# S4D convolution plus Mish feed-forward on one Trainium2 core: a new order for the first three chunks of block 0

## The chip, the core and the metric

The kernel runs on one core of a Trainium2 chip. A core has a matrix engine (PE; its weight loads are listed as PEld), a vector engine (DVE), an activation engine (ACT), a general engine (POOL) and a sync engine (SP) that mainly issues DMAs. Each engine works through its own instruction stream in order; semaphores tie the streams together. Matrix products end in PSUM, everything else lies in SBUF. The metric is the device time of one execution in microseconds. A time is the median of several runs, and one more execution is profiled; all traces here come from such a profiled execution.

## The reference

The input `A_u` is 2048 rows of 640. It is normalized per row, and three terms are added: the input itself, a diagonal state-space convolution with a skip term, and a dense layer pair with Mish between.

```python
x = A_u
xn = _layernorm(x, axis=-1)
return x + _A_ref(xn, ...) + _B_ref(xn, B_w1, B_b1, B_w2)

def _B_ref(x, w1, b1, w2):
    h = jnp.einsum("bsd,df->bsf", x, w1) + b1
    sp = jnp.log1p(jnp.exp(-jnp.abs(h))) + jnp.where(h > 0, h, jnp.zeros_like(h))
    act = h * jnp.tanh(sp)
    return jnp.einsum("bsf,fd->bsd", act, w2)
```

The inner width of the dense pair is 1728. The work in question is the beginning of `_layernorm` and of the first `einsum`.

## The kernel before

**Tiling.** The 2048 rows are four blocks of 512. A block has four tiles of 128 rows, numbered 0 to 3. The 640 columns are five slices `k`, the 1728 inner columns 14 chunks `f` (thirteen of 128, one of 64). PE multiplies 16-bit floats: each 32-bit operand is split into a rounded part, "high", and the residual, "low", and a product of two operands is made of three: high x high (`hh`), low weights x high input (`lh`), high weights x low input (`hl`). A chunk of the first layer thus has 15 products 512 columns wide, or 30 of half that width, called halves below; `CA` is the first half of a block's columns (tiles 0 and 1), `CB` the second (tiles 2 and 3).

**Two regimes.** From chunk 3 of block 0 on, a planner (`Plan`) orders all engines. It gets an estimated start time per engine, costs, predecessors and due times, and lets each engine take what is ready and due. PE's own order is that in which its operations were added. A predecessor that already has an entry in `pl.end` is dropped when an operation is added (`add`, line 89). The beginning, chunks 0, 1 and 2 of block 0, is an order written out by hand under `tc.manual_schedule()` (lines 1253 to 1334): each engine gets its instructions in the order of the calls.

**The steps of the beginning.** For every tile `i` of block 0:
- the tile is loaded to `X0`: tiles 0 and 1 as two column halves, one on SP's queue and one on ACT's (1256, 1257), tiles 2 and 3 as two halves of 64 rows on the same two queues (`load_x0`, 1245)
- DVE makes the statistics, two passes over half the columns each and a merge (`stat_ops`, 625), adds the epsilon (1280), and POOL raises the variance to the power -0.5 (1281)
- DVE subtracts the mean and multiplies (`norm0`, 1220); a variant on ACT, `norm0_a` (1223), exists but is not called
- PE transposes the five slices into PSUM (`to_t0`, 1235), slice 4 first.

For each half of the columns and each slice ACT copies the transposed input to 16 bits (`hi0`, 1239) and DVE makes the residual (`lo0`, 1242). For each chunk, `load_w1` (533) brings the weights, ACT rounds them (`hi_w1`, 550) and DVE makes their residual (`lo_w1`, 554). `mm1_part` (784) then issues products for a chunk, a list of kinds, a half and a list of slices. PE also runs 11 products of no use at the start (`fill`, 1249). In the old order chunks 1 and 2 do their low-weight products over all 512 columns at once.

**Loads.** Those of the weights of chunks 0 and 1 are split between SP's and ACT's queues as are those of all four tiles; ACT issues six DMAs before its first activation `warm` (1266), which makes it load its function tables. The rest goes out on SP.

**What follows.** Chunk 3 of the first layer is the first product at line 807, and after it PE alternates second-layer products (859) with further chunks. The first second-layer products wait for the activation of chunk 0: sigmoid (890), product with the input (894), arctangent, square and hyperbolic tangent on ACT (898, 902, 906), product (910) and split (916, 926).

Of the kernel before, what the change touches and what calls it, by code (L numbers as in the profile page):

```python
# [16 lines left out]
AF = mybir.ActivationFunctionType  # L17
OP = mybir.AluOpType
AX = mybir.AxisListType

P = 128
L = 2048
# [3 lines left out]
TB = 512  # L26
NB = L // TB
NT = TB // P
KD = D // P
# [9 lines left out]
EPS = 1e-5  # L39
# [10 lines left out]
SX, S1, SA, S2 = 2.0 ** 8, 2.0 ** 14, 2.0 ** 8, 2.0 ** 16  # L50
# [402 lines left out]
def body(ctx: ExitStack, tc: tile.TileContext, x, xT, logA, Aim, Cr, Ci, logdt, vec, w1, w1T, w2, w2T, out):  # L453
    nc = tc.nc
    v, a, pe, sp, g = nc.vector, nc.scalar, nc.tensor, nc.sync, nc.gpsimd
    xr = x[0].rearrange("(b i p) d -> b i p d", b=NB, i=NT, p=P)
# [10 lines left out]
    row = pool("row", 1)  # L467
# [11 lines left out]
    half, one, pi4, mb, zero = (kc[:, i:i + 1] for i in range(5))  # L479
    warm = kc[:, 5:6]  # L480
# [25 lines left out]
    CA, CB = slice(0, TB // 2), slice(TB // 2, TB)  # L506
# [10 lines left out]
    ACC = [ps.tile([P, TB], F32, name=f"acc{k}") for k in range(KD)]  # L517
    XT, ACT, SM, NX = ({} for _ in range(4))
    NCHK = NF + 3 * KD
    pl = Plan({"PE": 20.8, "ACT": 16.1, "DVE": 17.9, "SP": 15.0, "POOL": 15.0})  # L520
    tiles = lambda pool, name, n, shape: [pool.tile(shape, F32, name=f"{name}{j}") for j in range(n)]
    pl.pool("w", tiles(row, "w", 8, [P, D]))
    pl.pool("x", tiles(row, "x", 2, [P, D]))
# [9 lines left out]
    def load_w1(f, queues=(sp,)):  # L533
        t = kf(pl["w1", f])
        n, m = FC[f], P // len(queues)
        for j, e in enumerate(queues):
            o = D * FO[f] + j * m * KD * n
            e.dma_start(t[j * m:(j + 1) * m, :, :n], w1[o:o + m * KD * n].rearrange("(p k f) -> p k f", p=m, k=KD))
# [11 lines left out]
    def hi_w1(f):  # L550
        n = FC[f]
        a.activation(W1H[f][:, :, :n], kf(pl["w1", f])[:, :, :n], AF.Copy, scale=S1)

    def lo_w1(f):
        n = FC[f]
        v.scalar_tensor_tensor(W1L[f], kf(pl["w1", f])[:, :, :n], S1, W1H[f][:, :, :n], op0=OP.mult, op1=OP.subtract)
# [68 lines left out]
    def stat_ops(mv, xt, i):  # L625
        st = tmp.tile([P, 2, 6], F32, name="st", bufs=2)
        yield lambda: v.bn_stats(st[:, 0], xt[:, 0:320])  # L627
        yield lambda: v.bn_stats(st[:, 1], xt[:, 320:640])  # L628
        yield lambda: v.bn_aggr(mv[:, i], st)
# [154 lines left out]
    def mm1_part(f, kinds, c, start=False, stop=False, ks=range(KD)):  # L784

        ops = {"hh": (W1H[f], XH[0]), "lh": (W1L[f], XH[0]), "hl": (W1H[f], XL[0])}
        seq = [(ops[o], k) for k in ks for o in kinds]
        for j, ((w, x), k) in enumerate(seq):
            pe.matmul(bank(0, f)[:, c], w[:, k], x[k][:, c], start=start and j == 0, stop=stop and j == len(seq) - 1)  # L789
# [146 lines left out]
    def whole():  # L936

        A, V, M, S, G = "ACT", "DVE", "PE", "SP", "POOL"
        M5, M2 = 0.2157, 0.11
# [45 lines left out]
            return ops  # L985

        for f in range(3):
            pl.end["m1", 0, f] = (16.95, 18.55, 20.75)[f]


        for f in range(NF):
            if f > 5:
                add(("lw1", f), S, 0.1, load_w1, f, take=("w", ("w1", f), 1), kb=327.0)
            if f > 3:
                add(("hw1", f), A, 0.65, hi_w1, f, pre=[("lw1", f)] if f > 5 else [])
                add(("ow1", f), V, 0.75, lo_w1, f, pre=[("hw1", f)], drop=[("w1", f)])
            if f > 1:
                add(("lw2", f), S, 0.1, load_w2, f, take=("w", ("w2", f), 1), kb=327.0)
            add(("hw2", f), A, 0.65, hi_w2, f, pre=[("lw2", f)] if f > 1 else [])
# [17 lines left out]
        for b in range(1, NB):  # L1017
            for f in range(NF):
# [13 lines left out]
                i = PAIRS.index(f)  # L1032
                c = b
                one, two, three_a, three_b, four = mm1_pair(b, f)
# [12 lines left out]
                A2, B2 = second(*g2, [9] if FC[g2[1]] == P else [6]), second(*h2, [3, 9] if FC[h2[1]] == P else [2, 6])  # L1047
# [25 lines left out]
        b, k = NB - 1, KD - 1  # L1073
        two, one = LAST - 2, LAST - 1
# [25 lines left out]
        start = lambda b, f: at.get(("m1", b, f)) or at.get(("one", b, f)) or (start(b, f - 1) if f else pl.t["PE"] - 3.0)  # L1100

        for c in range(1, NB):
            b = c - 1
            t0 = start(b, 0)
            for i in range(NT):
                add(("lx", c, i), S, 0.1, lambda c=c, i=i: sp.dma_start(pl["x", c, i], xr[c, i]),
                    pre=[("st", c, i - 2)] if i > 1 else [], take=("x", ("x", c, i), 1), rel=t0, kb=327.0)
                add(("st", c, i), V, 1.1, stats, c, i, pre=[("lx", c, i)] + [("st", c, i - 1)] * (i > 0), drop=[("x", c, i)])
            add(("rs", c), G, 2.6, rstds, pre=[("st", c, NT - 1)])
            add(("sr", c), A, 0.25, spread_a, pre=[("spread", c)])  # L1110
            add(("sd", c), S, 0.1, spread_d, pre=[("sr", c)], kb=4.0)
            add(("bc", c), S, 0.2, spread_l, c, pre=[("sd", c)], take=("b", ("b", c), 2 * KD), kb=512.0)
# [103 lines left out]
    X0 = big.tile([P, NT, D], F32, name="x0", tag="bigA")  # L1216
    mv0 = tmp.tile([P, NT, 2], F32, name="mv0")
    rs0 = tmp.tile([P, 2, NT], F32, name="rs0")

    def norm0(i):  # L1220
        v.tensor_scalar(X0[:, i], X0[:, i], mv0[:, i, 0:1], rs0[:, 0, i:i + 1], op0=OP.subtract, op1=OP.mult)

    def norm0_a(i):
        v.scalar_tensor_tensor(rs0[:, 1, i:i + 1], mv0[:, i:i + 1, 0], -1.0, rs0[:, 0, i:i + 1], op0=OP.mult, op1=OP.mult)
        a.activation(X0[:, i], X0[:, i], AF.Identity, bias=rs0[:, 1, i:i + 1], scale=rs0[:, 0, i:i + 1])


    KS = (KD - 1, *range(KD - 1))
# [6 lines left out]
    def to_t0(i):  # L1235
        for k in KS:
            pe.transpose(flat0(k, (CA, CB)[i // 2])[:, i % 2 * P:(i % 2 + 1) * P], X0[:, i, k * P:(k + 1) * P], ident)  # L1237

    def hi0(k, c):
        a.activation(XH[0][k][:, c], flat0(k, c), AF.Copy, scale=SX)  # L1240

    def lo0(k, c):
        v.scalar_tensor_tensor(XL[0][k][:, c], flat0(k, c), SX, XH[0][k][:, c], op0=OP.mult, op1=OP.subtract)

    def load_x0(i):
        for e, c in ((sp, slice(0, P // 2)), (a, slice(P // 2, P))):
            e.dma_start(X0[c, i], xr[0, i, c])

    def fill(n):
        for _ in range(n):  # L1250
            pe.matmul(TR[:, 0:P], ident, ident, start=True, stop=True)

    with tc.manual_schedule():

        for i in range(2):
            sp.dma_start(X0[:, i, 0:320], xr[0, i, :, 0:320])
            a.dma_start(X0[:, i, 320:D], xr[0, i, :, 320:D])  # L1257
        for f in range(6):
            pl.take("w", ("w1", f))
            if f < 2:  # L1260
                pl.take("w", ("w2", f))
        load_w1(0, (sp, a))
        load_x0(2)
        load_w1(1, (sp, a))
        load_x0(3)
        a.activation(warm, one, AF.Sigmoid)
        load_w1(2)
        sp.dma_start(cv[:, 0:24], vec)
        load_w1(3)
        load_w2(0)  # L1270
        load_w1(4)
        load_w2(1)
        load_w1(5)
        S = [list(stat_ops(mv0, X0[:, i], i)) for i in range(NT)]

        def stats0(i):
            for o in S[i]:
                o()
            r = rs0[:, 0, i:i + 1]
            v.tensor_scalar(r, mv0[:, i:i + 1, 1], EPS, None, op0=OP.add)  # L1280
            g.tensor_tensor(r, r, half, op=OP.pow)

        fill(11)
        stats0(0)
        stats0(1)
        norm0(0)
        to_t0(0)
        hi_w1(0)
        norm0(1)
        to_t0(1)  # L1290
        for k in KS:
            hi0(k, CA)
        lo_w1(0)
        stats0(2)
        mm1_part(0, ("hh", "lh"), CA, start=True, ks=KS)
        hi_w1(1)
        lo0(KS[0], CA)
        lo0(KS[1], CA)
        mm1_part(1, ("hh",), CA, start=True)
        for f in range(2):  # L1300
            mm1_part(f, ("hl",), CA, ks=KS[:2])
        hi_w1(2)
        stats0(3)
        norm0(2)
        mm1_part(2, ("hh",), CA, start=True)
        to_t0(2)
        lo0(KS[2], CA)
        norm0(3)
        lo0(KS[3], CA)
        lo0(KS[4], CA)  # L1310
        mm1_part(2, ("hl",), CA, ks=KS[:2])
        for f in range(3):
            mm1_part(f, ("hl",), CA, ks=[KS[2]])
        to_t0(3)
        for k in KS[3:]:
            for f in range(3):
                mm1_part(f, ("hl",), CA, stop=f == 0 and k == KS[4], ks=[k])
        for k in KS:
            hi0(k, CB)
        lo_w1(1)  # L1320
        hi_w1(3)
        mm1_part(0, ("hh", "lh"), CB, start=True, ks=KS)
        for k in KS:
            lo0(k, CB)
        mm1_part(1, ("hh",), CB)
        mm1_part(0, ("hl",), CB, stop=True, ks=KS)
        lo_w1(2)
        lo_w1(3)
        for f in (1, 2):
            if f > 1:  # L1330
                mm1_part(f, ("hh",), CB)
            mm1_part(f, ("hl",), CB)
            mm1_part(f, ("lh",), slice(0, TB), stop=True)
        a.activation(bs, cv[:, 0:NF], AF.Copy, scale=SH)

    main.enter_context(tc.manual_schedule())
    for f in range(4):
        pl.drop(("w1", f), 17.0)
    whole()
    pl.run()  # L1340
    rv = NX.get("rv")
# [31 lines left out]
```

## Time and profile before

| | us |
|---|---|
| median of three runs | 358.29 |
| lowest and highest | 358.18, 358.57 |
| the profiled execution | 358.46 |
| its span in the trace | 356.6 |
| first transpose of a tile starts | 6.73 |
| first product of chunk 3 starts | 20.71 |

The span runs from the first to the last instruction of the trace; 1.86 us of the profiled execution lie outside it. Times in the trace count from the start of the span. A timeline row gives start and length in us, engine, line, operation, written and read tiles, shapes, and in brackets how long the engine sat idle before and what released it. A row "xN" merges N instructions. Products are pipelined on PE: one that is listed with 0.27 us follows another within less, so rows of PE overlap.

### The profile page before, as it was taken

How to read it: one execution, taken by the hardware profiler on the slowest of the kernel's cores; microseconds unless marked ns; L12 is line 12 of the kernel's file. 1: busy time of each engine (PE TensorE's matmuls, PEld its weight loads, DVE VectorE, ACT ScalarE, POOL GpSimd, SP SyncE). 2: the span in 40 equal slices, each digit the busy share in tenths (PEclk: the TensorE clock that was granted, in tenths of full speed). 3: DMA queues.
4: the chain of work that ended last, by engine and by line, in shares of the span. 5: the costliest groups of instructions: out<-in, count | busy, mean ns of one | idle time of the engine just before them, and what ended most of it. 6: DMA issues, size and time to landing. Idle time of an engine off the chain costs nothing.

```text
span 356.6 us, 6179 instructions
## 1 busy us (share of the span) xinstructions
PE 350.0 (98%) x2243; PEld 213.9 (60%) x2243; DVE 307.5 (86%) x585; ACT 293.8 (82%) x618; POOL 49.2 (14%) x72
## 2 busy tenths in 40 slices
PE   6999999999999999999999999999999999999996
PEld 6754445444666666675566666566566666667543
DVE  5989989999999999999999877799988878895552
ACT  3599999967698699999899977989989979877650
POOL 2100020000014231100003441000002443000000
PEclk9999999999999999999999999999999999999999
DMA  7879973301938935820444972841100994131004
GB/s 229 289 240 289 343 244 113 107 0 54 310 92 143 227 108 124 342 63 3 129 152 80 264 193 79 278 155 36 32 0 5 148 232 101 20 60 32 2 2 152
DMA packets 26052, 48.75 MB, mean 137 GB/s; under 512 B 3592, under 2 KB 6944, under 8 KB 26016
## 3 DMA queue, kind: packets, MB, share of 16 engines
q1 hardware_dynamic: 19168, 34.21, 29.5%
q0 software_dynamic: 6240, 13.11, 18.5%
q10 hardware_dynamic: 608, 0.98, 0.8%
q8 instruction: 19, 0.31, 0.3%
q14 instruction: 17, 0.14, 0.1%
HBM read 39.10 MB, written 5.26 MB: 124 GB/s over the span
## 4 chain that ended last, share of the span: by engine, by line
PE 96%; DMA 2%; DVE 1%; issue 0%; ACTq 0%; ACT 0%
PE acc L859 48%; PE h L827 18%; PE h L807 12%; PE tr L827 12%; PE h L800 2%; DMA w<-in_w_dram 2%; PE h L789 1%; PE tr L789 1%; PE acc L1237 0%; DVE st L627 0%; PE acc L871 0%; PE acc L870 0%; PE acc L873 0%; ACTq L1257 0%; DVE st L628 0%
## 5 line engine op out<-in xcount | busy, mean ns | idle before, releaser
L859 PE MATMUL acc<-hi,w2h 128*128 128x512 f16 x273 | 100.9, 379 | 0.0
L859 PE MATMUL acc<-hi,w2l 128*128 128x512 f16 (+1 forms) x265 | 99.7, 379 | 0.0
L859 PE MATMUL acc<-lo,w2h 128*128 128x512 f16 x253 | 93.3, 379 | 0.0
L859 PEld LDWEIGHTS <-w2h 128*128 128x128 f16 x526 | 50.9, 98 | 48.3 <-issue 1.9
L890 ACT ACTIVATE s<-h,cv 128x512 f32<-128x512 f32 (+1 forms) x55 | 32.7, 595 | 28.3 <-PE h L827 21.7
L827 PEld LDWEIGHTS <-w1h 128*128 128x128 f16 x432 | 42.3, 98 | 10.6
L910 DVE SCALAR_TENSOR_TENSOR A<-p,A 128x512 f32<-128x512 f32 (+1 forms) x56 | 37.4, 667 | 8.5 <-ACT p L906 7.9
L859 PEld LDWEIGHTS <-w2l 128*128 128x128 f16 x273 | 25.6, 98 | 30.8 <-issue 1.1
L926 DVE SCALAR_TENSOR_TENSOR lo<-A,hi 128x512 f16<-128x512 f32 x52 | 35.5, 683 | 8.1 <-ACT hi L916 8.0
L902 ACT ACTIVATE p<-p,kc 128x512 f32<-128x512 f32 (+1 forms) x56 | 39.3, 702 | 0.6
L898 ACT ACTIVATE p<-s,kc 128x512 f32<-128x512 f32 (+1 forms) x56 | 39.2, 701 | 0.5
L894 DVE SCALAR_TENSOR_TENSOR A<-h,bs,s 128x512 f32<-128x512 f32 (+1 forms) x55 | 35.0, 639 | 5.3 <-ACT s L890 5.2
L906 ACT ACTIVATE p<-p,kc 128x512 f32<-128x512 f32 (+1 forms) x56 | 39.2, 700 | 0.4
L916 ACT ACTIVATE hi<-A 128x512 f16<-128x512 f32 x52 | 32.4, 624 | 2.1 <-DVE A L910 1.9
L548 POOL DMA_DIRECT2D r<-in_xT_dram x15 | 13.4, 1011 | 132.2 <-DVE r L768 125.4
L749 DVE TENSOR_TENSOR_SCAN g<-g,car,kc 128x512 f32<-128x512 f32 x20 | 25.6, 1282 | 1.7 <-ACT g L743 1.6
L827 PEld LDWEIGHTS <-w1l 128*128 128x128 f16 x216 | 21.1, 98 | 8.2
L753 DVE TENSOR_TENSOR_SCAN g<-g,car,g 128x512 f32<-128x512 f32 x20 | 25.5, 1277 | 0.0
L827 PE MATMUL tr<-xh,w1l 128*128 128x256 f16 x90 | 24.5, 273 | 0.0
L827 PE MATMUL tr<-xh,w1h 128*128 128x256 f16 x90 | 24.5, 273 | 0.0
L827 PE MATMUL tr<-xl,w1h 128*128 128x256 f16 x90 | 24.5, 273 | 0.0
L827 PEld LDWEIGHTS <-swh 128*128 128x128 f16 x216 | 21.1, 98 | 4.4
(175 smaller groups left out, 718.9 us busy)
## 6 DMA issues: line engine op xcount, KB each, us to landing
w<-in_w_dram SPq DMA_DIRECT2D x23, 320.0 KB, 3.3
w<-in_w2T_dram SPq DMA_DIRECT2D x15, 288.0 KB, 6.1
w<-in_B_w_dram SPq DMA_DIRECT2D x13, 320.0 KB, 3.2
w<-in_w1T_dram SPq DMA_DIRECT2D x13, 320.0 KB, 6.6
x<-in_A_u_dram SPq DMA_DIRECT2D x12, 320.0 KB, 5.3
xt<-in_xT_dram SPq DMA_DIRECT2D x15, 256.0 KB, 5.6
r<-in_xT_dram POOLq DMA_DIRECT2D x15, 256.0 KB, 5.5
xt<-r POOLq DMA_DIRECT2D x15, 256.0 KB, 4.3
```

The source lines that it names most:

```text
L749: v.tensor_tensor_scan(g1[:, 1:], g1[:, 1:], zero.to_broadcast([P, TB]), car[:, 1, k:k + 1], op0=OP.add, op1=OP.add)
L807: pe.matmul(o, w, x, start=(j == 0), stop=(j == len(order) - 1))
L827: pe.matmul(o, p, q, start=start and n == 1, stop=n == 3 * len(w), skip_group_check=True)
L859: pe.matmul(o, w, x, start=start, stop=stop)
L890: a.activation(pl["s", b, f][:, c], bank(b, f)[:, c] if h is None else h, AF.Sigmoid, bias=cv[:, f:f + 1], scale=1 / SH)
L894: v.scalar_tensor_tensor(pl["A", b, f][:, c], bank(b, f)[:, c] if h is None else h, bs[:, f:f + 1], pl["s", b, f][:, c], op0=OP.add, op1=O ...
L898: a.activation(pl["p", b, f][:, cols(f)], pl["s", b, f][:, cols(f)], AF.Arctan, bias=one, scale=-1.0)
L902: a.activation(p, p, AF.Square, bias=pi4, scale=2.0)
L906: a.activation(p, p, AF.Tanh, bias=mb, scale=MG)
L910: v.scalar_tensor_tensor(A, pl["p", b, f][:, cols(f)], MC, A, op0=OP.add, op1=OP.mult)
L916: a.activation(hi, A, AF.Copy, scale=MA * SA / SH)
L926: v.scalar_tensor_tensor(lo, A, MA * SA / SH, hi, op0=OP.mult, op1=OP.subtract)
```

## The change

All engines get a new order for chunks 0 to 2, as one string that is read word by word. `S`, `M`, `N`, `A`, `T`, `H`, `L` with a number are the steps of a tile or chunk: statistics (two passes), moments (merge, epsilon, power), normalization on DVE, normalization on ACT, transposes, rounded weights, residual weights. `h` or `l` with a slice and a half is `hi0` or `lo0`. A word that begins with a digit is a chunk with its kinds of products, a slice and a half, so `1lhhl3a` is two halves of chunk 1. The text below names steps by these words (N0, A2, L1, h0b, l3b), for the old order too.

Tiles 0 and 2 are normalized on ACT; their bias, minus mean times power, is made by POOL behind the power. The residual of the input, the rounded weights and the products take new places, and every product is a half. The loads behind tiles 0 and 1 are whole and all on SP's queue, in the order weights of chunk 0, tile 2, weights of chunk 1, tile 3, weights of chunk 2 and so on. `warm` follows ACT's two remaining DMAs. The planner's start times for PE, ACT and DVE, three entries of `pl.end` and the time at which weight buffers count as free are new constants.

```diff
-    pl = Plan({"PE": 20.8, "ACT": 16.1, "DVE": 17.9, "SP": 15.0, "POOL": 15.0})
+    pl = Plan({"PE": 20.05, "ACT": 15.5, "DVE": 17.0, "SP": 15.0, "POOL": 15.0})
...
-            pl.end["m1", 0, f] = (16.95, 18.55, 20.75)[f]
+            pl.end["m1", 0, f] = (16.7, 17.95, 20.1)[f]
...
     def norm0_a(i):
-        v.scalar_tensor_tensor(rs0[:, 1, i:i + 1], mv0[:, i:i + 1, 0], -1.0, rs0[:, 0, i:i + 1], op0=OP.mult, op1=OP.mult)
         a.activation(X0[:, i], X0[:, i], AF.Identity, bias=rs0[:, 1, i:i + 1], scale=rs0[:, 0, i:i + 1])
...
-    def load_x0(i):
-        for e, c in ((sp, slice(0, P // 2)), (a, slice(P // 2, P))):
-            e.dma_start(X0[c, i], xr[0, i, c])
...
+    ORDER = ("S0 M0 S1 M1 A0 H0 N1 T0 T1 L0 h4a h0a S2 0hhlh4a h1a 0hhlh0a h2a 0hhlh1a H1 l4a 0hhlh2a M2 0hl4a h3a "
+             "l1a 1hh0a 1hh1a 1hh2a H2 l2a 0hh3a 0hl1a 0lh3a S3 1hl1a 0hl2a 1hl2a 1hh3a 1hhhl4a A2 2hh0a 2hh1a M3 "
+             "2hl1a 2hhhl2a L1 2hh3a 2hh4a H3 2hl4a T2 l3a 1lh0a 1lh1a N3 1lh2a 0hl3a 1lhhl3a 1lh4a l0a 2hl3a T3 "
+             "L3 h0b 0hl0a 1hl0a 2hl0a h3b 0hh0b l0b 0lh0b h2b 1hh0b 0hh3b l3b 0lh3b h4b 0hl0b 0hh2b l2b 0lh2b h1b "
+             "0hl3b 0hh4b l4b 0lh4b 0hhlh1b l1b 0hl2b 0hl4b 1lh0b L2 1hl0b 1hh1b 0hl1b 1lhhl1b 1hhlhhl2b 1hhlhhl3b "
+             "1hhlhhl4b 2lh0a 2lh1a 2lh2a 2lh3a 2lh4a 2hhlhhl0b 2hhlhhl1b 2hhlhhl2b 2hhlhhl3b 2hhlhhl4b")
+
+    def statistics(i):
+        S[i] = list(stat_ops(mv0, X0[:, i], i))
+        S[i][0]()
+        S[i][1]()
+
+    def moments(i):
+        S[i][2]()
+        r = rs0[:, 0, i:i + 1]
+        v.tensor_scalar(r, mv0[:, i:i + 1, 1], EPS, None, op0=OP.add)
+        g.tensor_tensor(r, r, half, op=OP.pow)
+        if "A%d" % i in ORDER:
+            g.tensor_scalar(rs0[:, 1, i:i + 1], mv0[:, i:i + 1, 0], -1.0, r, op0=OP.mult, op1=OP.mult)
+
+    def products(s):
+        f, k, half = int(s[0]), int(s[-2]), s[-1]
+        kinds = [s[i:i + 2] for i in range(1, len(s) - 2, 2)]
+        start = (f, half) not in count
+        count[f, half] = count.get((f, half), 0) + len(kinds)
+        mm1_part(f, kinds, CA if half == "a" else CB, start=start, stop=count[f, half] == 3 * KD, ks=[k])
...
+        a.activation(warm, one, AF.Sigmoid)
...
-        load_w1(0, (sp, a))
-        load_x0(2)
-        load_w1(1, (sp, a))
-        load_x0(3)
-        a.activation(warm, one, AF.Sigmoid)
+        for i in range(2):
+            load_w1(i)
+            sp.dma_start(X0[:, i + 2], xr[0, i + 2])
...
+        S, count = {}, {}
+        act = {"S": statistics, "M": moments, "N": norm0, "A": norm0_a, "T": to_t0, "H": hi_w1, "L": lo_w1}
+        row = {"h": hi0, "l": lo0}
+        for s in ORDER.split():
+            if s[0].isdigit():
+                products(s)
+            elif s[0] in row:
+                row[s[0]](int(s[1]), CA if s[2] == "a" else CB)
+            else:
+                act[s[0]](int(s[1]))
...
-        pl.drop(("w1", f), 17.0)
+        pl.drop(("w1", f), 16.9)
```

The hand-written sequence of the old order, lines 1274 to 1333, goes.

More of the change, by code (lines that the diff above doesn't have):

```diff
@@ L1273, in body @@
         load_w1(5)
[L1274 to L1281, printed above, removed]
-        fill(11)
[L1284 to L1333, printed above, removed]
+        fill(11)
+        S, count = {}, {}
[8 more added lines that the diff above has]
+                act[s[0]](int(s[1]))
         a.activation(bs, cv[:, 0:NF], AF.Copy, scale=SH)
```

## The prediction

> **What bounds the kernel now.** I read the page first (its first part and the busy tenths), then the windows of the head, then the timeline of the first 24 us. In the page the reader is to see that PE is nearly the whole span and that its strip has one weak digit at each end.
>
> ```profile
> span 356.6 us, 6179 instructions
> ...
> PE 350.0 (98%) x2243; PEld 213.9 (60%) x2243; DVE 307.5 (86%) x585; ACT 293.8 (82%) x618; POOL 49.2 (14%) x72
> ...
> PE   6999999999999999999999999999999999999996
> ```
>
> The windows (length, then busy time of PE, PEld, DVE, ACT, POOL, then clock, DMA share, GB/s) put all of PE's idleness before 16 us, apart from the last output; after that busy equals length. So the end is the start of that unbroken stretch plus fixed work, and only what moves its start, or tears a hole in it, moves the end.
>
> ```profile
> 6.73:12.00 5.27, 4.64 (x34) 3.10 (x34) 4.61 (x13) 3.58 (x8) 1.03 (x3) 1.00 0.96 283
> 12.00:16.00 4.00, 3.86 (x36) 3.35 (x34) 3.89 (x10) 2.16 (x7) 0.73 (x1) 1.00 0.89 335
> 16.00:20.71 4.71, 4.71 (x35) 3.26 (x34) 4.07 (x7) 3.64 (x7) 0.00 (x0) 1.00 0.68 199
> 20.71:40.00 19.29, 19.29 (x91) 8.80 (x90) 18.18 (x35) 19.29 (x34) 0.00 (x0) 1.00 0.92 297
> ```
>
> The timeline (start, length, engine, line, operation) shows where the head waits: for the normalized tiles, for ACT's copies and for weights.
>
> ```profile
> 6.73 0.76 PE L1237 MATMUL acc<-ident,x 128*128 128x128 f32 x5 [0.95 <-DVE x L1221]
> 7.80 0.77 PE L1237 MATMUL acc<-ident,x 128*128 128x128 f32 x5 [0.31 <-DVE x L1221]
> 8.16 1.49 ACT L1240 ACTIVATE xh<-acc 128x256 f16<-128x256 f32 x5 [0.33 <-PE acc L1237]
> 8.60 0.27 PE L789 MATMUL h<-xh,w1h 128*128 128x256 f16 x1
> 10.32 0.72 PE L789 MATMUL h<-xh,w1h 128*128 128x256 f16 x5 [0.24 <-ACT w1h L552]
> 12.38 0.77 PE L1237 MATMUL acc<-ident,x 128*128 128x128 f32 x5
> 13.53 0.71 PE L1237 MATMUL acc<-ident,x 128*128 128x128 f32 x5
> 16.37 1.25 PE L789 MATMUL h<-xl,w1h 128*128 128x256 f16 x10
> 20.71 1.24 PE L807 MATMUL h<-xh,w1h 128*128 128x512 f16 x5
> ```
>
> Ten half-wide products take 1.25, the last 0.27 of it, so one follows the other by 0.109. Five transposes in a row take 0.58 of PE, halfway between the spacings of 6.73 and 13.53. The three chunks are 90 halves and 20 transposes: 9.81 + 2.32 = 12.13. From 6.73 to 20.71 are 13.98, so 1.85 is idle. That is the most the new order can win with T0 where it is.
>
> **The change part by part.** *Opening: tile 0 goes to ACT.* N0 on DVE needed only the power; A0 on ACT also needs a bias, made by one more POOL operation.
>
> ```profile
> 5.01 0.57 POOL L1281 TENSOR_TENSOR rs<-rs,kc 128x1 f32<-128x1 f32 x1 [3.52 <-DVE rs L1280]
> 6.00 0.15 DVE L1280 TENSOR_SCALAR rs<-mv 128x1 f32<-128x1 f32 x1
> 6.07 0.60 DVE L1221 TENSOR_SCALAR x<-x,mv,rs 128x640 f32<-128x640 f32 x1
> 6.23 0.86 POOL L1281 TENSOR_TENSOR rs<-rs,kc 128x1 f32<-128x1 f32 x1 [0.65 <-DVE rs L1280]
> 7.10 0.74 ACT L552 ACTIVATE w1h<-w 128x640 f16<-128x640 f32 x1 [0.44 <-DMA w<-in_w_dram]
> L633 POOL TENSOR_SCALAR st_row<-mv x3: 229/349/562, 44.9 to 211.2; 128x4 f32<-128x4 f32 x3
> L898 ACT ACTIVATE p<-s,kc 128x512 f32<-128x512 f32 x2 | 1.4, 713 | 0.0
> 22.60 0.62 ACT L916 ACTIVATE hi<-A 128x512 f16<-128x512 f32 x1
> ```
>
> The trace has no such bias operation. The nearest is POOL's TENSOR_SCALAR, 0.23 to 0.56; I take its median, 0.35, and keep both ends. It runs 5.67 to 6.02. A0 is a 640-wide activation (0.74) with two operands read per partition; one such operand costs 0.09 (0.71 at L898 against 0.62 at L916, both 512 wide), so 0.92: 6.07 to 6.99. T0 starts at 7.04, 0.31 **later** than now. Tile 1 gains: its power began at 6.23 and took 0.86 beside N0; alone I take 0.57, as at 5.01. N1 runs 6.84 to 7.45, and T1 starts when T0 is through, 7.65, against 7.80. ACT's first copy follows T1 by 0.36 as now: 8.01 against 8.16. Only 0.15 is won here. ACT's table load has no part in it: ACT now issues two DMAs ahead of it, not six, and it ends long before 6.07.
>
> *The middle, to T2.* ACT's copies come every 0.275 ((1.49 - 0.39) / 4), so the fifth step, H1, runs 9.11 to 9.85; the products paced by the copies end near 9.5, and chunk 1 starts at 9.90 (10.32 now). Behind it stand 20 halves whose operands are then there or arrive in step: 12.10.
>
> ```profile
> 7.87 0.82 DVE L556 SCALAR_TENSOR_TENSOR w1l<-w,w1h 128x640 f16<-128x640 f32 x1
> 8.61 0.49 DVE L627 BATCH_NORM_STATS2 st<-x 128x6 f32<-128x320 f32 x1
> 9.84 0.74 DVE L1243 SCALAR_TENSOR_TENSOR xl<-acc,xh 128x256 f16<-128x256 f32 x2
> ```
>
> DVE: H0 follows A0 on ACT at 6.89 (its transfer must have landed) and ends at 7.63; L0 starts at 7.66, S2 at 8.40 (0.74 later, as 7.87 to 8.61). From S2 to the end of tile 2's epsilon is 1.23 now; with l4a (0.33) put between, l1a starts at 9.87. POOL's power (0.55) and bias (0.35) for tile 2 end by 11.02, A2 on ACT runs 11.07 to 11.99, T2 could start at 12.04: just hidden behind PE's 12.10. A0 and A2 are new waits on ACT for POOL: behind A0 stand H0 and the copies, behind A2 H3 and T3's copies. Had A2 no cover, each 0.1 of it would cost 0.1. T2 and eight halves take PE to 13.55.
>
> *T3.* Behind l1a and l2a (0.33 each) S3 starts on DVE at 10.53. 1.23 later, at 11.77, L1 starts, to 12.59; tile 3's epsilon comes 0.07 ahead of it (as 6.00 before 6.07), while POOL's power for tile 3 is only asked for at about 11.93. What does such a neighbour cost?
>
> ```profile
> 10.00 0.55 POOL L1281 TENSOR_TENSOR rs<-rs,kc 128x1 f32<-128x1 f32 x1 [2.90 <-DVE rs L1280]
> 45.26 0.82 DVE L556 SCALAR_TENSOR_TENSOR w1l<-w,w1h 128x640 f16<-128x640 f32 x1
> 45.52 1.50 POOL L634 TENSOR_TENSOR st_row<-st_row,kc 128x4 f32<-128x4 f32 x1
> 211.63 1.04 POOL L634 TENSOR_TENSOR st_row<-st_row,kc 128x4 f32<-128x4 f32 x1
> ```
>
> The same instruction, L556, ran ahead of a four-element power at 45.52, which took 1.50 instead of 1.04 and ended 0.94 after L556. The single power at 6.23 ended 0.42 after N0 (7.09 against 6.67). At 10.00, beside a residual from PSUM, it took 0.55. So I take that it ends 0.42 after L1: 13.01, not 12.48. N3 runs 13.05 to 13.65 and T3 starts at 13.70: PE idles 0.15. [...]
>
> *From T3.* The order has 37 halves before T3 and 53 behind it. ACT's copies from T3 (0.275 apart) feed two to four halves each and DVE's residuals stay ahead (the tightest, l3b, ends at 15.40 for a use at 15.48), so none is waited for: 13.70 + 0.58 + 53 x 0.109 = 20.06 for the first L807 product, against 20.71. **Shift: 0.65 earlier.** The second-half products of the third kind, 512 wide before, are two halves now: same columns, and the weight loads (0.10) fit under 0.109.
>
> *Loads.*
>
> ```profile
> 3.60 0.47 SPq L538 DMA_DIRECT2D w<-in_w_dram  x1
> 7.09 0.33 SPq L538 DMA_DIRECT2D w<-in_w_dram  x1
> 10.73 0.74 ACT L552 ACTIVATE w1h<-w 128x640 f16<-128x640 f32 x1 [0.46 <-DMA w<-in_w_dram]
> DMA packets 555, 0.65 MB, mean 163 GB/s; under 512 B 54, under 2 KB 546, under 8 KB 555
> 14.00:15.00 1.00, 1.00 (x12) 0.90 (x11) 1.00 (x3) 1.00 (x5) 0.00 (x0) 1.00 1.03 410
> ```
>
> Today eight transfers are issued at once; the ninth (3.60) waits for a landing, and w1 of chunk 2 for w1 of chunk 0 (7.09, landed 10.71). With whole tiles that one is itself the ninth issue and goes out near 3.6. By 4.0 us 0.65 MB, the first two tiles, had moved. The five loads behind them are 1.64 MB; at 283 GB/s they are in by 9.8. H2 may start as late as 10.4 (its first product comes at 11.21), so this is hidden by 0.6 or less.
>
> *Downstream.* PE's order is fixed; the other engines' starts in the plan move by 0.6 to 0.9, nearly together, and the three ends given to the plan are inert, since `add` drops a predecessor that already has an end.
>
> ```profile
> 17.12 0.69 ACT L890 ACTIVATE s<-h,cv 128x512 f32<-128x512 f32 x1 [1.07 <-PE h L789]
> 23.95 0.38 PE L859 MATMUL acc<-hi,w2h 128*128 128x512 f16 x1
> ```
>
> The nearest wait is that of 23.95 for the activation of chunk 0, ready at 23.22. Chunk 0 now has 31 halves behind its last, so ends at 16.68 against 16.92: ready at 22.98, while PE asks at 23.30. It stays hidden by 0.32.
>
> **The sum.** The profiled execution took 358.46 (span 356.6 and 1.86 around it): 357.81. The median shown is 0.17 lower, so the forecast is 358.29 - 0.65 = 357.64. About 0.2%, 0.72 us, is what a measurement of this kernel can tell from no change; the forecast lies just inside. With the bias at 0.23 everything moves 0.12 earlier (357.52), at 0.56 0.21 later (357.85).
>
> **The rivals.**
> - *No exclusion at T3.* If the power runs beside L1, T3 starts at 13.55: 357.49, or 357.37 with the short bias. The rows at 10.00 (for) and 45.52 (against) decide; the second is the same L556.
> - *Weights of chunk 2 no earlier than now.* Landing at 10.71 lets H2 end at 11.46 and PE resume at 11.51 instead of 11.21; 0.15 of it vanishes in T3's wait: 357.79. For it: transfers now take 3.6 from issue to landing and share all engines. Against: its issue is 3.5 earlier. The same for chunk 0's weights (landed 7.08 now, wanted at 6.89) would move L0 and T3 by about 0.2: 357.84.
> - *The win is given back at 23.95.* ACT is full from 20.71 to 40. If the shifted plan puts one more activation (0.62 or so) ahead of that of chunk 0, 0.30 comes back: 357.94.
> - *Slower: one queue feeds too little.* Everything in order waits for H2. From a landing at 10.4 on each microsecond costs one, less 0.15; from about 11.9, a mean of 208 GB/s behind the tiles, the result is over 0.2% slower. At the 199 GB/s of the last window of the head it lands at 12.24: 357.64 + 1.69 = 359.33. Against: 410 GB/s at 14 us, when SP alone issues. [...]
>
> **Chances.** Forecast with its bounds 0.42 (0.12 of it beyond 0.2% faster), no exclusion 0.25, late weights 0.15, given back 0.12, starved queue 0.06. Faster by over 0.2%: 0.12 + 0.25 = 0.37; slower 0.06; within 0.57. The range, 357.2 to 358.2, holds all but the last and part of the tails.
>
> **What will show it.** T0 near 7.04 and T1 near 7.65; ACT's first copy near 8.0; chunk 1's first product near 9.9; the fourth power about 1.1 long, ending 0.4 after L1; T3 near 13.7 with a short wait for DVE; no DMA wait at H2; the first sigmoid near 16.9; the first L807 product near 20.06, and no PE idleness behind it until the last output. A wait of PE after 20 us, or one of ACT for a transfer, makes the forecast wrong.

## The result and the profile after

The changed kernel is slower, not faster: 359.81 us (median, 359.61 to 360.13) against 358.24 for the kernel before in the same comparison, a ratio of 1.0041 with a 95% interval of 1.0029 to 1.0054. The forecast of 357.64 and its range up to 358.2 were wrong. The profiled execution took 359.66 us with a span of 357.9; before it was 358.46 with 356.6.

The page of the changed kernel does not show at once where 1.3 us of span have gone. Its first part and the strip of PE's busy tenths:

```profile
span 357.9 us, 6182 instructions
...
PE 350.5 (98%) x2253; PEld 215.5 (60%) x2253; DVE 305.9 (85%) x583; ACT 295.3 (83%) x620; POOL 48.8 (14%) x74
...
PE   7999999999999999999999999999999999999994
```

The first digit went up from 6 to 7, the last one down from 6 to 4: the beginning is better, and the end is worse. The windows of the changed kernel (length, busy time of PE, PEld, DVE, ACT, POOL, then clock, DMA share, GB/s) confirm the first half of that. Against before PE is busy for 4.98 of the first 5.27 us, not 4.64, and it again has no hole from 16 us on:

```profile
6.73:12.00 5.27, 4.98 (x40) 3.84 (x41) 4.98 (x14) 4.68 (x11) 1.07 (x4) 1.00 1.02 389
12.00:16.00 4.00, 3.99 (x35) 3.16 (x33) 3.77 (x9) 1.95 (x7) 0.83 (x1) 1.00 1.00 367
16.00:20.16 4.16, 4.16 (x41) 3.71 (x39) 3.38 (x6) 3.19 (x6) 0.00 (x0) 1.00 0.53 190
20.16:40.00 19.84, 19.84 (x94) 9.00 (x92) 18.77 (x36) 19.84 (x34) 0.00 (x0) 1.00 0.85 252
40.00:345.00 305.00, 305.00 (x1987) 186.93 (x1986) 268.10 (x502) 263.37 (x563) 44.63 (x59) 1.00 0.46 120
```

The timeline of the changed kernel's beginning (start, length, engine, line, operation, idle time before and releaser):

```profile
5.65 0.26 POOL L1269 TENSOR_SCALAR rs<-mv,rs 128x1 f32<-128x1 f32 x1
5.95 0.92 ACT L1224 ACTIVATE x<-x,rs 128x640 f32<-128x640 f32 x1 [2.80 <-DVE mv L629]
6.93 1.31 PE L1236 MATMUL acc<-ident,x 128*128 128x128 f32 x10 [0.48 <-ACT x L1224]
7.84 1.21 ACT L1239 ACTIVATE xh<-acc 128x256 f16<-128x256 f32 x4 [0.34 <-PE acc L1236]
9.72 0.61 PE L789 MATMUL h<-xh,w1h 128*128 128x256 f16 x4
9.80 0.77 ACT L552 ACTIVATE w1h<-w 128x640 f16<-128x640 f32 x1
10.82 0.92 ACT L1224 ACTIVATE x<-x,rs 128x640 f32<-128x640 f32 x1 [0.26 <-POOL rs L1269]
11.61 0.82 DVE L556 SCALAR_TENSOR_TENSOR w1l<-w,w1h 128x640 f16<-128x640 f32 x1
11.78 1.05 POOL L1267 TENSOR_TENSOR rs<-rs,kc 128x1 f32<-128x1 f32 x1 [0.99 <-DVE rs L1266]
11.94 0.71 PE L1236 MATMUL acc<-ident,x 128*128 128x128 f32 x5
13.53 0.53 PEld L1236 LDWEIGHTS acc<-ident,x 128*128 128x128 f32 x5 [0.29 <-DVE x L1221]
16.97 0.69 ACT L890 ACTIVATE s<-h,cv 128x512 f32<-128x512 f32 x1 [1.27 <-PE h L789]
20.16 1.24 PE L807 MATMUL h<-xh,w1h 128*128 128x512 f16 x5
23.39 0.38 PE L859 MATMUL acc<-hi,w2h 128*128 128x512 f16 x1
```

Read the last two against before: chunk 3 begins 0.55 us earlier (20.16, 20.71 before), and the first product of the second layer 0.56 earlier (23.39, 23.95), without a wait. The whole stream behind keeps this. The last product and the last addition to the output, in the timeline of before and then of after:

```profile
352.85 0.27 PE L881 MATMUL h<-lo,w2h 128*128 128x256 f16 x1
353.16 0.42 DVE L933 SCALAR_TENSOR_TENSOR xt<-h,xt 128x256 f32<-128x256 f32 x1 [0.56 <-PE h L881]
```

```profile
352.30 0.27 PE L881 MATMUL h<-lo,w2h 128*128 128x256 f16 x1
352.61 0.42 DVE L933 SCALAR_TENSOR_TENSOR xt<-h,xt 128x256 f32<-128x256 f32 x1 [0.56 <-PE h L881]
```

So at the last arithmetic of the kernel the change is still 0.55 us ahead. It loses 1.85 us of span behind it, where the kernel stores the last output, waits for every transfer and lets the five engines meet twice before it ends. All that belongs to one line. The view of that line lists the closing instructions of each queue with count, duration in ns, and the start of the first and of the last. Before, then after:

```profile
L1369 PEldq DRAIN  x2: 8/8/8, 355.1 to 356.1; - x2
L1369 ACTq EVENT_SEMAPHORE  x2: 17/17/17, 355.9 to 356.5; - x2
L1369 PEldq EVENT_SEMAPHORE  x2: 51/51/51, 355.9 to 356.5; - x2
```

```profile
L1344 PEldq DRAIN  x2: 8/8/8, 354.5 to 357.6; - x2
L1344 ACTq EVENT_SEMAPHORE  x2: 17/17/17, 356.0 to 357.8; - x2
L1344 PEldq EVENT_SEMAPHORE  x2: 51/51/51, 357.5 to 357.8; - x2
```

Before, PE's two events (355.9, 356.5) come with ACT's. After, PE's own first drain is done 0.5 earlier (354.55 against 355.07), but its first event comes at 357.5, 1.5 us behind ACT's at 356.0, though PE has had nothing to compute for five microseconds. This is the first loss. The second is that ACT's event, which only waits for the common start of the meeting, comes at 356.0 instead of 355.9, although the last output was ready 0.55 earlier. SP's waits (who was waited for, us in total, times, longest), before and after, show both:

```profile
SPq L1369 <- PEq L1369: 0.7, 2, 0.5
SPq L1369 <- DMA out_dram<-xt: 0.4, 2, 0.2
```

```profile
SPq L1344 <- PEq L1344: 1.8, 2, 1.5
SPq L1344 <- DMA out_dram<-xt: 1.1, 3, 0.5
```

**What PE waits for.** The instruction queue of the page carries 19 packets of 0.31 MB in both kernels, 16 KB each. Their starts in the trace are 14 to 27 us apart where PE works on products, and between two of these starts the trace of the changed kernel has 253 PE instructions on average (199 to 303); without the last of these stretches, which ends at the block of the closing jump, it has 4096 in sixteen (16.57 to 332.36), 256 each.

```profile
q8 instruction: 19, 0.31, 0.4%
```

So PE's program arrives in blocks of 16 KB, about 250 instructions; from these counts an instruction is estimated at 64 or 65 bytes. The last block but one comes at PE's closing jump, over the branch for general inputs that is not taken here (the jump is 3.84 us long before and 3.87 after, and ends 1.51 and 1.53 behind the end of its block's transfer), the last one behind it. Worked out from the trace's transfers and events, in us:

| kernel | last 16 KB transfer | PE's first closing event | ACT's first |
|---|---|---|---|
| before | 355.53 to 356.55 | 355.92 | 355.91 |
| after | 355.03 to 356.01 | 357.48 | 356.00 |

Before, the event runs while the last transfer is still on its way: it lies in the block ahead. After, it comes 1.47 behind the transfer's end, nearly the delay that the jump shows. The reading is that the change moved PE's closing code across the limit of a block, by 20 more products and loads (2253 of each, 2243 before) less two events (8, 10 before): 18 instructions.

**What SP waits for.** SP's last duty is a list of twelve waits in both kernels, on the semaphores in use. The transfers of SP's and ACT's queues take turns at eight of these (in the trace of before 16 transfers on each of 100 and 102 to 108). Starts of the waits, the landing of the last output (semaphore in brackets) and POOL's event that opens the meeting:

```
before  ... 354.63 (103)  355.02 (104)  355.10 (105)  355.16 (106)  355.39 (107)  355.62 (108)  POOL 355.78
        last output: semaphore 108, landed 355.60
after   ... 354.91 (103)  355.10 (104)  355.16 (106)  355.25 (107)  355.64 (108)  355.72 (109)  POOL 355.87
        last output: semaphore 104, landed 355.09
```

The change issues four transfers fewer (four whole ones for eight halves). So the last output falls on semaphore 104 instead of 108, and behind its wait four more are still to be passed, one of which stands 0.39 after its neighbour. That pause is in the list of both kernels, but before it lies between the waits at 354.63 and 355.02, ahead of the last landing. From landing to POOL's event it is 0.18 before and 0.78 after: of 0.51 gained at the landing 0.60 is paid back.

### The profile page after: what moved, and what is told of

Its sections match the earlier page's. It is cut to its first block, busy times and chain, and to the rows that moved or that the text cites. A ratio compares the mean times of both kernels' runs of the same rounds, so it can differ in the third digit from the quotient of the medians.

```text
span 357.9 us, 6182 instructions
## 1 busy us (share of the span) xinstructions
PE 350.5 (98%) x2253; PEld 215.5 (60%) x2253; DVE 305.9 (85%) x583; ACT 295.3 (83%) x620; POOL 48.8 (14%) x74
## 3 DMA queue, kind: packets, MB, share of 16 engines
HBM read 39.10 MB, written 5.26 MB: 124 GB/s over the span
## 4 chain that ended last, share of the span: by engine, by line
PE 96%; DVE 1%; DMA 1%; ACT 0%; issue 0%
PE acc L859 48%; PE h L827 18%; PE h L807 12%; PE tr L827 12%; PE h L800 2%; PE h L789 2%; PE tr L789 1%; DMA x<-in_A_u_dram 1%; PE acc L1236 0%; DVE st L627 0%; DVE st L628 0%; ACT x L1224 0%; PE acc L873 0%; PE acc L870 0%; PE acc L871 0%; DVE w1l L556 0%
```

## The experiments

The theory of two losses: (1) the limit of a 16 KB block in PE's closing code, which makes PE's event about 1.5 us late; (2) the order of SP's closing list, about 0.6 us, as much as the gain. Rivals: the new order itself costs time that the trace puts at the end; products of half width cost something; the loss goes with the four fewer transfers alone.

**PE's code moved and nothing else.** The branch for general inputs is compiled into the program but not taken. Idle products in it, `n` pairs of product and load, lengthen PE's program ahead of the closing code, and none is executed:

```diff
         make_identity(nc, ident)
+        ih = ident.bitcast(F16)
+        idle = ps.tile([P, P], F32, name="f_idle")
+        for _ in range(n):
+            pe.matmul(idle, ih[:, 0:P], ih[:, 0:P], start=True, stop=True)
         kc = one.tile([P, 5], F32, name="f_kc")
```

The kernel before with ten pairs, `before_gen20`:

> The kernel before, with 20 PE instructions added inside the general path, which is never taken; what runs is unchanged, but PE's closing instructions lie 20 places further back in its code, as in the changed kernel. Code theory (the loss sits behind the last output: PE fetches one more block of code between its last drain and the closing barrier): PE's work stays where it was (first L807 product at 20.7, last product at 352.9), the gap between PE's last drain and the barrier event grows from 0.85 to about 2.9 us, and the time rises by 1.2 to 1.6 us, to about 359.7. Rival (the new order, its plan or its DMA lanes make the end late): nothing changes, 358.2 within 0.3.

It was not late: 358.29 us, ratio 0.9999 (0.9989 to 1.0009), span 356.5. The count was off: 20 is the number of added products and loads, but two events went, so the change moves the code by 18. The kernel before with nine pairs, `before_gen18`:

> The kernel before, with 18 PE instructions added inside the general path, which is never taken. The changed kernel's PE executes 10 products and 10 weight loads more than before but 2 semaphore instructions fewer, so its closing code lies 18 places further back, not 20. Code theory, refined (only where the 16 KB limit falls between PE's last drain and the barrier event does PE wait for a block): exactly this shift is late, PE's barrier event 1.5 us behind the other engines', 359.7 to 360.0. Rival (the lateness belongs to the new order, and the paddings of the changed kernel removed it by some other shift): as before, 358.3 to 358.5.

360.02 us, ratio 1.0043 (1.0027 to 1.006). The same closing line of this kernel, then of the one with 20:

```profile
L1373 PEldq DRAIN  x2: 8/8/8, 354.9 to 357.9; - x2
L1373 ACTq EVENT_SEMAPHORE  x2: 17/17/17, 355.8 to 358.1; - x2
L1373 PEldq EVENT_SEMAPHORE  x2: 51/51/51, 357.8 to 358.1; - x2
```

```profile
L1373 PEldq DRAIN  x2: 8/8/8, 355.0 to 356.0; - x2
L1373 PEldq EVENT_SEMAPHORE  x2: 51/51/51, 355.9 to 356.5; - x2
```

The kernel before, with not one executed instruction changed, becomes as slow as the changed kernel, and two instructions more make it fast again. Eighteen plus one block, `before_gen274`, and eighteen less two, `before_gen16`, test the period and the place of the limit:

> The kernel before with 274 idle PE instructions (137 pairs) in the branch that is never taken: 18, which made it late, plus 256, the number of PE instructions between two of the 16 KB instruction transfers. If the loss is set by where PE's closing code lies against the limits of such 16 KB blocks, the time is again near 360.0, span 358.2, PE's closing event some 2 us behind the other engines'. If it is set by the length of the code or by something that 18 instructions changed once, the time is that of before, 358.3 to 358.6.

> The kernel before with 16 idle PE instructions. 18 was late and 20 was not, so the limit lies at or just ahead of PE's first closing event at 18. Two instructions fewer put the limit between PE's first and second closing event. If the wait for the transfer goes with the limit, the first event is in time (355.9) and the second one is late instead, at about the same absolute time as with 18 (near 357.8, where before has 356.5): span near 357.9, time near 359.7. If only that one position is bad, the time is that of before, 358.3 to 358.6.

With 274 it is 360.15 us, ratio 1.0048 (1.0031 to 1.0065), PE's first event 2.05 behind ACT's (357.97 against 355.92): a period of 256 fits, and so does the mean of 253 instructions between two transfers. With 16 it is 359.88, ratio 1.0044 (1.003 to 1.0059), and the closing line of that kernel shows the first event in time and the second one late:

```profile
L1373 ACTq EVENT_SEMAPHORE  x2: 17/17/17, 355.5 to 356.1; - x2
L1373 PEldq EVENT_SEMAPHORE  x2: 51/51/51, 355.5 to 357.8; - x2
```

The wait goes with the limit from one instruction to the next. In the changed kernel the same move must take the loss away. Two instructions in the branch, 40 and 236 were tried; with the 18 of the change they shift PE's closing code by 20, 58 and 254, so 236 leaves it two short of a whole block:

> The changed kernel with 2 PE instructions added inside the general path, which is never taken: a shift of 20 against the kernel before, which was harmless there. Refined code theory: the late barrier event is gone, 358.5 to 358.6 as with 40 and 236. Rival (a wider band of positions is late): 359.8.

> The changed kernel, with 40 PE instructions added inside the general path, which is never taken. Code theory: the block limit now lies ahead of the target of PE's closing jump, so that the block fetched for the jump holds all that follows; no late barrier event, 357.7 to 358.2. If instead any shift beyond that of the kernel before costs the same (not a limit that is crossed, but code that is further away), 359.8. Rival (order, plan, lanes): 359.8 as well.

> The changed kernel, with 236 PE instructions added inside the general path, which is never taken. Together with the 20 that the change adds these are 256 of 64 bytes, one block of 16 KB, so PE's closing instructions stand in their block as in the kernel before. Code theory: head and stream as in the changed kernel (L807 at 20.16, last product at 352.3), no late barrier event of PE, time 358.24 - 0.55 = 357.7, at most 358.2 if the sync engine's own last waits stay as late as in the changed kernel. Rival (order, plan, lanes): 359.8 as the changed kernel.

They took 358.5, 358.57 and 358.56 us, ratios 0.9996 (0.9986 to 1.0005), 1.0003 (0.9993 to 1.0012) and 1.0003 (0.9994 to 1.0013), with spans of 356.6 and 356.7. PE's first event again comes 0.01 behind ACT's (356.046 against 356.038 with 236). The first loss is gone in all three, and none is faster than before, against the forecast for 40 and 236: the second one is still there, and it eats the gain. SP's waits of the kernel with 40 have the first row of before and the second of after:

```profile
SPq L1348 <- DMA out_dram<-xt: 1.1, 3, 0.5
SPq L1348 <- PEq L1348: 0.7, 2, 0.5
```

**Products of half width.** The kernel before with the low-weight products of chunks 1 and 2 in halves, `before_halves`, executes the same 20 instructions more:

```diff
-            mm1_part(f, ("lh",), slice(0, TB), stop=True)
+            mm1_part(f, ("lh",), CA)
+            mm1_part(f, ("lh",), CB, stop=True)
```

> The kernel before, with only the low-weight products of chunks 1 and 2 of block 0 issued as halves: 10 products of 512 columns become 20 of 256, so PE executes 20 instructions more and the same columns. Code theory: the stream stays within 0.1 us of before, and the end is late as in the changed kernel: about 359.7. Rival (halves are harmless, the order is what costs): 358.2 within 0.3. If the halves themselves cost PE time, the first L807 product moves from 20.71 by that much.

358.43 us, ratio 0.9998 (0.9988 to 1.0009). The halves cost nothing, and 20 executed instructions, like 20 that are not executed, do not hit the limit.

**SP's closing list.** Four more transfers in the middle of the kernel put the last output back on the last semaphore of the list. Five loads of parameters are cut into nine:

```diff
-            for k in (slice(0, KD),) if j < 3 else (slice(0, 3), slice(3, KD)):
+            for k in (slice(0, 3), slice(3, KD)) if j < 3 else (slice(0, 2), slice(2, 4), slice(4, KD)):
```

In the changed kernel with 40 idle instructions, `after_gen40_dma4`:

> The changed kernel with 40 PE instructions in the path that is never taken, and the five loads of the convolution's parameters cut into nine, so four more DMAs are issued, which puts back the four that the change saved at the start. Lane theory (the DMAs take turns at eight semaphores; the sync engine waits for these in a fixed order at the end; with four DMAs fewer the last output's semaphore is no longer the last in that order, and four further waits and a fixed 0.39 us pause stand behind its landing): the last landing ends the waits again, the span is 356.1 and the time 0.5 below the kernel before. Rival (the 0.55 us are lost in the new order or in the output itself): 358.5 as without the four.

357.86 us, ratio 0.9981 (0.9971 to 0.9991), span 356.0. The last output lands at 355.02, POOL's event is at 355.20, and SP's row for the output is that of before again:

```profile
SPq L1348 <- PEq L1348: 0.7, 2, 0.5
SPq L1348 <- DMA out_dram<-xt: 0.4, 2, 0.2
```

In the kernel before the same four transfers move the last output to another place, `before_dma4`:

> The kernel before with the five parameter loads cut into nine, four DMAs more. Lane theory: the last output's semaphore comes four places ahead of the end of the sync engine's list, so three or four more waits of 0.06 to 0.09 us follow its landing, and 0.39 more if the pause falls behind it: 0.2 to 0.6 us slower than before. Rival: no change.

358.54 us, ratio 1.0003 (0.9994 to 1.0013): no loss that can be measured in the time. From the last landing to POOL's event it is 0.42 (355.37 to 355.79) instead of 0.18, as the list says, but in that execution chunk 3 began at 20.40, 0.31 earlier than in the profile of before, with the order of the beginning untouched, and the 0.24 of the list lies inside it. The old beginning varies: in the executions of before and of its four padded versions chunk 3 began between 20.33 and 20.71. Part of this goes with the landing of the weights of chunk 2. In the profile of before ACT waits 0.46 for them and rounds them at 10.73. In `before_dma4` it rounds them straight behind those of chunk 1 (the second of two merged rows), and in `before_gen16`, where chunk 3 began at 20.33, after 0.19:

```profile
9.41 1.50 ACT L552 ACTIVATE w1h<-w 128x640 f16<-128x640 f32 x2
```

```profile
10.29 0.74 ACT L556 ACTIVATE w1h<-w 128x640 f16<-128x640 f32 x1 [0.19 <-DMA w<-in_w_dram]
```

What else moves it stays open. In six executions of the new order (the changed kernel and its versions with other padding or transfers) chunk 3 began between 20.12 and 20.21.

Last, the four transfers in the changed kernel without any padding, `after_dma4`:

> The changed kernel with five whole-chunk loads cut into nine parts (four more DMAs), so that the last output gets the last place in SP's closing list again, but without any padding of PE's code. If the two losses at the end are independent, only the list is mended: PE's closing event still comes about 1.5 us behind the other engines', and the time is 357.86 (the same with 40 idle instructions) plus 1.5, near 359.3; span near 357.5. If the two are one loss (the DMAs alone would do), the time is near 357.9. If the cut loads and not the padding had moved the code, PE's event comes with the others.

359.58 us, ratio 1.0032 (1.0019 to 1.0045), span 358.1; the forecast of 359.3 was 0.3 low. ACT's event now comes at 355.46, PE's at 357.68, again 1.47 behind the end of its transfer (356.21). So the two losses are not a sum. The meeting begins with the later of the two, and PE's event follows its own transfer: with the limit in the wrong place SP's list costs nothing, and mending it brings nothing that can be told from the variation of that transfer (0.98 long in the changed kernel, 1.18 here).

The stretch from the start of the last addition to the end of the span leaves the variation of the beginning out. It sorts the kernels by what is late at their end:

| late at the end | kernels | us |
|---|---|---|
| nothing | `before`, `before_gen20`, `before_halves`, `after_gen40_dma4` | 3.41 to 3.48 |
| the list | `before_dma4` | 3.74 |
| the list | `after_gen2`, `after_gen40`, `after_gen236` | 4.05 to 4.08 |
| PE's event | `before_gen16`, `before_gen18`, `before_gen274`, `after_dma4` | 5.05 to 5.42 |
| both | the changed kernel | 5.26 |

So the 0.33 that the list costs in `before_dma4` is there, inside the forecast 0.2 to 0.6, and PE's late event by itself lengthens the end by 1.6 to 2.0 us.

**The order at T3.** The prediction counted a cost for L1 beside POOL's fourth power. In `lock_free`, built on `after_gen40_dma4`, L1 goes behind N3, and DVE makes residuals from PSUM in its place:

```diff
-             "2hl1a 2hhhl2a L1 2hh3a 2hh4a H3 2hl4a T2 l3a 1lh0a 1lh1a N3 1lh2a 0hl3a 1lhhl3a 1lh4a l0a 2hl3a T3 "
-             "L3 h0b 0hl0a 1hl0a 2hl0a h3b 0hh0b l0b ... "
+             "2hl1a 2hhhl2a l3a l0a 2hh3a 2hh4a H3 2hl4a T2 0hl3a 1hl3a 2hl3a N3 L1 0hl0a 1hl0a 2hl0a T3 "
+             "L3 h0b 1lh0a 1lh1a 1lh2a 1lh3a 1lh4a h3b 0hh0b l0b ... "
```

> The version with 40 idle instructions and four more DMAs, and in the order the residual weights of chunk 1 (L1) moved behind the normalization of tile 3 (N3), the two PSUM residuals l3a and l0a in its place, and six high-weight low-input halves ahead of T3 instead of the five low-weight ones, which come behind it. If it is L1's two SBUF operands that hold up POOL's power for tile 3 (1.05 long in the changed kernel, ending 0.40 after L1), the power takes 0.55 to 0.57 here and ends near 12.35, N3 ends near 13.0, T3 follows PE's six halves near 13.2 without a wait for DVE, and the first product of chunk 3 comes 0.2 to 0.35 earlier than 20.16, the time at 357.5 to 357.7. If any DVE work beside it slows the power, it takes about 1.0 again, T3 stays near 13.5 and the time at 357.86. If what is won at T3 is lost behind it (the residual weights come later), the first product of chunk 3 stays near 20.1 with an idle stretch of PE between 13.8 and 16.

357.55 us, ratio 0.998 (0.997 to 0.999), span 355.7: faster than both kernels. Against `after_gen40_dma4` the span is 0.3 shorter, but the ratios of the two (0.998 and 0.9981) cannot be told apart, as the kernel before was 0.3 lower in this comparison, too. Its end is 3.42 long, as in `after_gen40_dma4`, so the 0.3 of the span lies in the beginning. The timeline of this kernel at the place:

```profile
11.62 0.75 DVE L1246 SCALAR_TENSOR_TENSOR xl<-acc,xh 128x256 f16<-128x256 f32 x2
11.79 0.55 POOL L1271 TENSOR_TENSOR rs<-rs,kc 128x1 f32<-128x1 f32 x1 [0.99 <-DVE rs L1270]
12.38 0.61 DVE L1225 TENSOR_SCALAR x<-x,mv,rs 128x640 f32<-128x640 f32 x1
13.15 0.71 PE L1240 MATMUL acc<-ident,x 128*128 128x128 f32 x5
19.79 1.24 PE L811 MATMUL h<-xh,w1h 128*128 128x512 f16 x5
```

The same power, issued at the same time (11.78 and 11.79), takes 0.55 beside work with one operand in PSUM and took 1.05 beside L1 with both in SBUF. T3 starts at 13.15 without a wait for DVE and chunk 3 at 19.79, 0.37 earlier than in the changed kernel and 0.33 earlier than in `after_gen40_dma4` (20.12), well outside the spread of the new order's six executions.

## Why the prediction was wrong

The mechanism at the beginning was right, nearly number by number, and the failure lies outside of it.

- **The failed step** is the first one and the sum that rests on it: "the end is the start of that unbroken stretch plus fixed work". The work behind the last product is not fixed: from the start of the last addition to the end of the span it took 3.41 us before and 5.26 after, and these 1.85 us outweigh the shift. (The 1.86 us outside the span did hold, at 1.79.) The last 3 us of the span were not read at all, neither for the sum nor for the list of what would show it right or wrong. Their rows were in the trace of before. PE's event stood 0.01 behind ACT's while a transfer of PE's code was under way, and the last output's wait was the last of SP's list. The part on loads looked at the fewer transfers only for what they do at the beginning; the remark that halves bring "same columns, and the weight loads (0.10) fit under 0.109" counted time and not instructions.
- **The shift** was forecast at 0.65 and is 0.55 between the two profiles. Up to T3 all came 0.11 to 0.18 earlier than forecast: the bias took 0.26, not 0.35 (a bound, 0.23, was nearer than the chosen median); A0 took the forecast 0.92; T0 began at 6.93 (7.04), chunk 1 at 9.72 (9.90), T2 at 11.94 (12.10) and T3 at 13.54 (13.70). That the total came so near is in part luck: 0.16 won up to T3 and 0.26 given back behind it partly cancel, and the start to be beaten, 20.71, was read from one execution at the late end of what the old order does. The mean of six executions of the old order is 20.55, that of six of the new one 20.17, only 0.38 apart.
- **Behind T3** 0.26 was given back. "None is waited for" was wrong by two short holes. The first, 0.09, is the wait for ACT's first copy from T3: it starts at 14.12 and is 0.39 long, and PE's product with it starts at 14.56. At the second, 0.14, the products of chunk 0 with the residual l3b, which was to end at 15.40, found it at 15.51. The timeline shows l3b as the first of the two rows at 15.09, 0.13 after the end of the one before it, and PE's product at 15.57; why DVE paused there stays open.

```profile
15.09 0.76 DVE L1242 SCALAR_TENSOR_TENSOR xl<-acc,xh 128x256 f16<-128x256 f32 x2
15.32 0.27 PE L789 MATMUL h<-xh,w1l 128*128 128x256 f16 x1
15.57 0.27 PE L789 MATMUL h<-xl,w1h 128*128 128x256 f16 x1
```

- **The power behind its neighbour at T3** was right: the fourth power is 1.05 long and ends 0.40 after L1 (12.83 against 12.43; 0.42 was taken). "No exclusion" falls, and `lock_free` shows what avoiding the neighbour gives: 0.33 at chunk 3 and 0.3 of the span, between single profiles. The power's end 0.40 behind L1 is 0.15 less than the 0.55 of a whole power in `lock_free`, so no run shows that L1 held it up for its whole length.
- **The loads** were hidden: H2 starts at 9.80 straight behind the copies. In other executions of the new order it waits up to 0.29 for its weights (10.28 in `after_gen236`), with chunk 3 at 20.20 all the same. The rivals of late weights and of one queue that feeds too little fall; from 6.73 to 12 us 389 GB/s were moved where before it was 283.
- **"Given back at 23.95"** falls too: 23.39 without a wait, the sigmoid at 16.97 (16.9 was forecast).
- **The rival on the slower side** named the wrong place. The true one, a limit in PE's program behind the last output, was not among the rivals.

Without both losses the change brings what its beginning shows: 357.86 against 358.6 in that comparison, 0.7 us, and by the interval of the ratio 0.3 to 1.0 us. Both 0.55, between the two profiles, and 0.38, between the means, lie in it.

## What to carry to other kernels

When all that is changed lies at the beginning and the engine in question is never idle again, the end still has to be read: compare the closing line of each engine, SP's list of waits and the last landing before calling the rest fixed. An edit that changes the number of PE's instructions, even ones that are not executed, moves all of PE's later code against the 16 KB blocks (by 18 here), so a loss of about 1.5 us at the end should be tested with a few idle instructions before the order itself is blamed. An edit that changes the number of transfers moves the last output to another place of the closing list (four fewer here, from the last place to the fifth from the end). And where the beginning varies from one execution to the next, a gain there should be measured against several traces and not one.

## What was not expected of the hardware

- PE's program comes in 16 KB blocks of about 256 instructions (18 idle instructions and 274 make the same loss, 20 none; in the changed kernel 253 on average lie between two transfers, 256 up to the block of the jump). When the limit falls between the closing jump and one of the two closing events, that event comes 1.35 to 1.62 us behind the end of the transfer (357.76 against 356.41 with 18, 357.78 against 356.16 with 16). The jump itself ends 1.51 to 1.53 behind the end of its block's transfer in all fourteen traces. The seventeen transfers ahead of it cost PE nothing that the windows show: in the changed kernel they start from 16.57 to 332.36, and PE is busy for 329.00 of the 329.00 us from 16 to 345.
- SP's list of closing waits takes 0.06 to 0.09 us a step where nothing is waited for and has one pause of 0.39 to 0.40 that moves with the number of transfers: it follows the seventh of the twelve waits before and the tenth after, with four transfers fewer. In all fourteen traces an 8 KB transfer of instructions (queue q14 of the page) starts 0.62 to 0.82 after the end of the pause. What makes the pause was not shown: no run tried it.
- A power of one element per partition on POOL takes 0.55 beside a DVE residual with one operand in PSUM and 1.05 beside one with both in SBUF. That it needs two operands is not shown: beside N0, which reads one tile and two columns from SBUF, it took 0.86 in the kernel before.
